# Copying the values' shifted halves on GpSimd instead of by DMA, in an attention kernel followed by a two-layer network

## The chip, the cores and the metric

The kernel runs on one core of a Trainium2 chip. The metric is the device time of one execution, in microseconds (us); a lower time is better. The core has TensorE (PE: matmuls; PEld: its weight loads), VectorE (DVE), ScalarE (ACT), GpSimd (POOL) and SyncE (SP). Transfers are issued from a queue of GpSimd or of SP and run on 16 DMA engines. The working memory (SBUF) has 128 partitions; matmul results lie in PSUM.

## The reference

There are 8 batches, 8 heads, 576 positions and a head size of 64. Heads 0 to 3 attend to the last 32 positions ("plain"); heads 4 to 7 to every fourth of the last 128 ("dilated"). The attention's output, 4608 rows of 512, goes through two matrices with a SiLU between them.

```python
scores = scale * np.matmul(q, k.transpose(0, 1, 3, 2))
rel = pos[:, None] - pos[None, :]
mask_plain = (rel >= 0) & (rel < 32)
mask_dil = (rel >= 0) & (rel < 128) & (rel % 4 == 0)
scores = np.where(masks, scores, -1e9)      # plain: h < 4, dilated: h >= 4
attn = exp(scores - max) / (sum + 1e-9)
x = np.matmul(attn, v)                      # -> (4608, 512)
h = x @ w_in                                # 512 x 2048
out = (h * sigmoid(h)) @ w_out              # 2048 x 512
```

## The kernel before, in words

**Work per batch.** The 576 queries of a head are cut into blocks of 32, each of which sees 64 keys: its own 32 and the 32 before. A dilated head is first split into its four classes of positions modulo 4, after which each class is a plain head of 144 positions. For one batch and one kind of head (z = 0 plain, z = 1 dilated) the steps are: scores (L362 plain, L374 dilated, small matmuls), mask and maximum (L486 to L512, VectorE), exp (L525, L534, ScalarE), normalisation (`normal`, L543 to L550, VectorE), transposing the weights (on TensorE, L559 and L567, or by DMA, L574), `values` (L601 and L665 on TensorE) and `finish`, which puts the result into xT. Then layer 1 (L691 with SiLU at L699) and layer 2 (L756) run over the batch, 16 tiles of the hidden size and 4 or 5 tiles of rows.

**Values.** The tile `vw`, of which there are two (batch b uses `vws[b % 2]`), holds v in pieces of 64 keys on partitions. `load_v` (L158 to L181) brings the pieces from HBM into partitions 64 to 127 (and a short tail). Each piece is needed a second time, shifted by 32 keys, in partitions 0 to 63. These shifted halves are made by `shift_v` (L200), out of four copies within `vw`, each of 32 partitions of 16-bit numbers:

- `shift_class` (L193): 2048 numbers per partition, dilated heads
- `shift_over` (L198): 1024, dilated heads
- `shift_plain` (L186, L188): 2304 and 2048, plain heads

The function is handed the operation that copies. Batch 0 has its own copies (some by DMA from SP, some on VectorE).

**Rows of q and k.** For batches 1 and 2 `load_qk` (L107) loads them and TensorE transposes them. From batch 3 on `load_rows` (L119 plain, L127 dilated; 12 issues on GpSimd) loads them and `cross` (L140, L147) transposes them by DMA, issued from SP.

**Order.** All engines work their own instructions in the order in which the program wrote them. The order is written out by hand in `plan_of(b)`: `at(s, f, ...)` runs f at step s of batch b, where steps 0 to 15 are the tiles of layer 1 and those from 16 the groups of four matmuls of layer 2. Loads of later batches are so placed between the matmuls of this one; the attention of batch b + 1 is computed during the layers of batch b. On GpSimd this gives, in b = 0: v of batch 1, `load_qk(2)` (L107), rows of batch 3, v of batch 2, its shift; in b = 1: v of 3, its shift, rows of 4; from b = 2: v of b + 2, its shift, rows of b + 3. A load of v into a buffer waits until TensorE has done with the batch before in it (L665 is its last use). Batch 1's shift is issued from SP.

Of the kernel before, what the change touches and what calls it, by code (L numbers as in the profile page):

```python
# [29 lines left out]
def kernel(  # L30
# [9 lines left out]
    nc = tc.nc  # L40
    B, H, S, D = q.shape
# [727 lines left out]
    def transposes(at, b, z, step):  # L769
        for which in (1, 0):  # L770
            at(step, transpose, b, z, which, both)

    def later(at, b, z, steps, copies=(nc.vector.tensor_copy, nc.vector.tensor_copy)):

        for hi in (0, 1):
            if steps[hi] is not None:
                at(steps[hi], normal, b, z, hi)
        for hi in (0, 1):
            at(steps[2], turn, b, z, hi)
        for hi in (0, 1):  # L780
            at(steps[2], turned, b, z, hi, copies[hi])
        at(steps[3], values, b, z)
        at(steps[3], finish, b, z, copies)

    def plan_of(b):
        ev = {}

        def at(s, fn, *args):
            ev.setdefault(s, []).append((fn, args))

        def all_exps(b, z):
            for hi in (0, 1):
                at(16, exps, b, z, hi)

        if b == 0:

            at(-16, normal, 0, 1, 1)
            at(-15, shift_class, 0, dve, 1, 2)
            at(-14, normal, 0, 0, 1)
            at(-13, clear_v, 1, nc.vector)  # L800
            at(-13, load_v, 1)
            for c in (2, 3):
                at(-13, load_w_out, c)
            at(-13, load_qk, 2)
            at(-8, turn, 0, 1, 1)
            at(-8, turned, 0, 1, 1, act)
            at(-6, values0, 1, 1)
            at(-6, last_values, 0, 1, (1,))
            at(-6, finish0, 1, 1)
            at(-6, last_finish, 0, 1, 1)  # L810
            at(-4, turn, 0, 0, 1)
            at(-4, turned, 0, 0, 1)
            at(-2, values0, 0, 1)
            at(-2, last_values, 0, 0, (1,))
            at(-2, finish0, 0, 1, both)
            at(-2, last_finish, 0, 0, 1)
            transposes(at, 1, 1, 2)
            at(8, scores, 1, 1)
            for hi in (0, 1):
                at(8, shift, 1, 1, hi)  # L820
            for which in (1, 0):
                at(17, transpose, 1, 0, which, (dve, dve))
            at(20, normal, 1, 1, 0)
            at(20, scores, 1, 0)
            at(14, shift_v, 1, nc.sync.dma_start)
            at(15, load_rows, 3)
            at(15, load_v, 2)
            at(15, shift_v, 2, nc.gpsimd.dma_start)
            all_exps(1, 1)
            for hi in (0, 1):  # L830
                at(20, exps, 1, 0, hi)
            for n, z, hi in ((20, 1, 1), (26, 0, 0), (28, 0, 1)):
                at(n, normal, 1, z, hi)
            for n, z, copies in ((27, 1, (dve, dve)), (30, 0, both)):
                for hi in (0, 1):
                    at(n, turn, 1, z, hi)
                for hi in (0, 1):
                    at(n, turned, 1, z, hi, copies[hi])
                at(n + 1 + z, values, 1, z)
                at(n + 1 + z, finish, 1, z, both)  # L840
        elif b == 1:
            transposes(at, 2, 0, 2)
            transposes(at, 2, 1, 11)
            at(2, cross, 3, 0)
            at(20, cross, 3, 1)
            at(28, cross, 4, 0)
            at(8, scores, 2, 0)
            for hi in (0, 1):
                at(8, shift, 2, 0, hi)
            at(17, load_v, 3)  # L850
            at(17, shift_v, 3, nc.gpsimd.dma_start)
            at(17, load_rows, 4)
            at(14, scores, 2, 1)
            all_exps(2, 0)
            all_exps(2, 1)
            for hi in (0, 1):
                at(21, normal, 2, 0, hi)
            at(21, scores, 3, 0)
            at(21, exps, 3, 0, 0)
            at(21, exps, 3, 0, 1)  # L860
            later(at, 2, 0, (None, None, 27, 28))
            later(at, 2, 1, (29, 31, 33, 34))
        else:
            if b + 2 < B:
                at(16, cross, b + 2, 1)
                at(16, load_v, b + 2)
                at(16, shift_v, b + 2, nc.gpsimd.dma_start)
            if b + 3 < B:
                at(16, load_rows, b + 3)
            if b + 1 < B:  # L870
                if b == 2:
                    later(at, 3, 0, (0, 0, 4, 6))
                else:
                    at(6, values, b + 1, 0)
                    at(6, finish, b + 1, 0)
                at(11, scores, b + 1, 1)
                at(11, shift, b + 1, 1, 1)
                all_exps(b + 1, 1)
            if b + 2 < B:
                at(17, scores, b + 2, 0)  # L880
                for hi in (0, 1):
                    at(18, exps, b + 2, 0, hi)
            if b + 1 < B:
                for hi in (0, 1):
                    at(22 + hi, normal, b + 1, 1, hi)
                    at(22 + hi, turn_by_dma, b + 1, 1, hi)
                at(29, values, b + 1, 1)
                at(29, finish, b + 1, 1)
            if b + 2 < B:
                for hi in (0, 1):  # L890
                    at(27 + hi, normal, b + 2, 0, hi)
                    at(27 + hi, turn_by_dma, b + 2, 0, hi)
            if b + 3 < B:
                at(31, cross, b + 3, 0)

        def plan(s):
            for fn, args in ev.pop(s, ()):
                fn(*args)

        return plan  # L900
# [58 lines left out]
    for b in range(B):  # L959
        plan = plan_of(b)  # L960
        if b == 0:
            for x in range(NFF):
                plan(2 * x - NFF)
                plan(2 * x + 1 - NFF)
                layer1_part(2 * x % NFF, 2 * x // NFF, None if x else warm)
        else:
            for f in range(NFF):
                plan(f)
                layer1(b, f)
        if b == 0:  # L970
            layer2_first(plan)
        else:
            layer2(b, plan)
        for s in range(NFF, 3 * NFF):
            plan(s)
# [30 lines left out]
```

## Time and profile before

| | |
|---|---|
| three runs | 314.29, 315.76, 318.0 us (median 315.76) |
| the profiled execution's own time | 316.22 us |
| its span, first to last instruction | 314.4 us |
| mean granted TensorE clock | 0.977 |
| DMA bytes in all | 41.27 MB, mean 131 GB/s |
| copies within vw, issued from GpSimd | 24 issues; 4.0 to 5.4 us to landing (medians) |
| copies within vw, issued from SP | 7 issues (3 of batch 0, 4 of batch 1); 5.3 to 6.5 us to landing |
| ScalarE, SiLU of layer 1 (L699) | 72.8 us busy |

"Busy" is the time in which an engine had an instruction under way. The chain is the sequence of work that ended last, followed back from the end; its "issue" entries are times in which the engine waited for nothing that the profile shows. In a timeline, `[2.65 <-DMA w_out...]` says that the engine sat idle 2.65 us before the row and what ended this. A queue's share is the time that its packets took, of 16 engines' span; packets of two queues overlap, so shares of a short stretch can add up to more than 100%.

### The profile page before, as it was taken

The page shows a single profiled execution, that of the slowest core. Times are in us where ns is not written, and L with a number is a line of the kernel's source. Part 1 is how long each engine was busy: PE and PEld are TensorE (multiplying, and loading weights), DVE is VectorE, ACT ScalarE, POOL GpSimd, SP SyncE. Part 2 cuts the span into 40 slices and gives each one's busy share as a digit, 9 for nine tenths or more (in the row PEclk, how much of TensorE's full clock was granted, in tenths as well). Part 3 has the DMA queues.
Part 4 walks back from the last instruction along what each step waited for, and adds up shares of the span by engine and source line. Part 5 has one row for each costly group of instructions (what it writes and reads, how often), then busy time and mean ns, then how long its engine had stood idle before and what let it go on. Part 6 is the DMA issues. An engine that isn't in the chain of part 4 may idle for free.

```text
span 314.4 us, 10401 instructions
## 1 busy us (share of the span) xinstructions
PE 298.6 (95%) x4465; PEld 191.3 (61%) x4465; DVE 166.0 (53%) x352; ACT 186.3 (59%) x554; POOL 102.7 (33%) x160
## 2 busy tenths in 40 slices
PE   5789999999999969999989999999999999999995
PEld 2458755677446846467644676467744676467544
DVE  5896588627697334841676126851587034520011
ACT  2775658766992537945694356955695448436300
POOL 8536537715584165056504183042000000000000
PEclk9679999999999989999999999999999999999999
DMA  8999999999999999399996999299715100310021
GB/s 108 188 212 205 191 230 172 170 186 139 171 171 166 189 141 124 93 162 199 123 145 139 176 207 123 76 159 174 106 56 127 67 4 0 109 69 2 0 102 68
DMA packets 105087, 41.27 MB, mean 131 GB/s; under 512 B 79248, under 2 KB 99600, under 8 KB 105040
## 3 DMA queue, kind: packets, MB, share of 16 engines
q0 software_dynamic: 64160, 21.73, 66.8%
q1 hardware_dynamic: 40736, 18.80, 29.2%
q8 instruction: 35, 0.57, 0.7%
q14 instruction: 12, 0.10, 0.1%
q10 hardware_dynamic: 144, 0.07, 0.1%
HBM read 37.75 MB, written 9.44 MB: 150 GB/s over the span
## 4 chain that ended last, share of the span: by engine, by line
PE 85%; DMA 5%; DVE 3%; ACT 3%; issue 2%; POOL 1%; POOLq 0%; DVEq 0%
PE h L691 34%; PE o L756 32%; PE o L730 5%; PE h L711 4%; PE x L601 3%; DMA ptT<-pn 3%; DMA n<-in_q_dram 2%; PE s L374 1%; PE s L362 1%; PE pt L559 1%; PE t L312 1%; ACT pe L534 1%; PE x L627 1%; POOL n L156 1%; DVE ob L740 1%
## 5 line engine op out<-in xcount | busy, mean ns | idle before, releaser
L699 ACT ACTIVATE gT<-h 128x576 f16<-128x576 f32 x112 | 72.8, 650 | 85.8 <-PE h L691 85.6
L691 PE MATMUL h<-xT,w_in 128*128 128x288 f16 x896 | 115.2, 289 | 0.0
L756 PE MATMUL o<-w_out,gT 128*128 128x512 f16 (+1 forms) x528 | 114.1, 373 | 0.0
L691 PEld LDWEIGHTS <-w_in 128*128 128x128 f16 x896 | 87.2, 99 | 24.3 <-DVE xT L678 0.3
L756 PEld LDWEIGHTS <-gT 128*128 128x128 f16 x528 | 50.6, 98 | 54.9
L534 ACT ACTIVATE pe<-ms,nm 128x64 f32<-128x64 f32 x178 | 59.1, 333 | 4.2 <-DVE nm L502 4.1
L740 DVE COPY ob<-o 128x512 f32<-128x512 f32 (+1 forms) x34 | 23.1, 681 | 51.8 <-PE o L756 51.0
L486 DVE SCALAR_TENSOR_TENSOR ms<-s,mask 128x512 f32<-128x512 f32 x28 | 19.2, 685 | 45.6 <-PE s L374 28.3
L534 ACT ACTIVATION_READ_ACCUMULATOR pe<-ms,nm 128x1 f32 x178 | 33.2, 186 | 0.0
L678 DVE CAST xT<-x 128x512 f16<-128x512 f32 x26 | 16.8, 684 | 27.9 <-PE xs L665 27.9
L550 DVE TENSOR_TENSOR pn<-pe,r 128x640 f16<-128x640 f32 (+2 forms) x32 | 25.3, 792 | 1.1
L165 POOL DMA_DIRECT2D vw<-in_v_dram x16 | 10.0, 638 | 44.8 <-PE xs L665 44.6
L502 DVE TENSOR_REDUCE nm<-ms 128x10 f32<-128x640 f32 (+1 forms) x28 | 22.0, 786 | 1.0
L711 PE MATMUL h<-xT,w_in 128*128 128x256 f16 (+1 forms) x128 | 17.4, 290 | 1.0 <-ACT gT L718 1.0
L119 POOL DMA_DIRECT2D n<-in_q_dram x20 | 14.8, 788 | 2.5 <-DMA vw<-vw 2.5
L711 PEld LDWEIGHTS <-w_in 128*128 128x128 f16 x128 | 12.3, 99 | 4.9 <-issue 1.7
L119 POOL DMA_DIRECT2D n<-in_k_dram x20 | 14.8, 759 | 1.4 <-issue 1.3
L730 PE MATMUL o<-w_out,gT 128*128 128x512 f16 x64 | 15.1, 380 | 0.0
L718 ACT ACTIVATE gT<-h 128x512 f16<-128x512 f32 (+1 forms) x16 | 10.3, 650 | 6.9 <-PE h L711 6.8
L601 PEld LDWEIGHTS <-vw 64*64 64x64 f16 x896 | 8.7, 108 | 5.8 <-issue 5.8
L601 PE MATMUL x<-ptT,vw 64*64 64x32 f16 x896 | 10.3, 187 | 0.7 <-DVE ptT L567 0.5
L740 ACT COPY ob_last<-o 128x128 f32<-128x128 f32 x1 | 0.3, 265 | 17.0 <-DMA out_dram<-ob 17.0
(108 smaller groups left out, 258.0 us busy)
## 6 DMA issues: line engine op xcount, KB each, us to landing
out_dram<-ob SPq DMA_DIRECT2D x35, 256.0 KB, 2.3
vw<-in_v_dram POOLq DMA_DIRECT2D x8, 288.0 KB, 8.4
vw<-in_v_dram POOLq DMA_DIRECT2D x16, 128.0 KB, 5.7
w_in<-in_moe_w_in_dram POOLq DMA_DIRECT2D x4, 512.0 KB, 11.8
w_out<-in_moe_w_out_dram POOLq DMA_DIRECT2D x4, 512.0 KB, 10.4
n<-in_k_dram POOLq DMA_DIRECT2D x6, 256.0 KB, 5.5
n<-in_q_dram POOLq DMA_DIRECT2D x6, 256.0 KB, 5.7
vw<-vw POOLq DMA_DIRECT2D x12, 128.0 KB, 4.7
```

What stands on the lines that cost most here:

```text
L119: nc.gpsimd.dma_start(out=f[:, h // 2, :, h % 2], in_=src[b, h].rearrange("(m p) d -> p m d", p=RT))
L486: nc.vector.scalar_tensor_tensor(out=ms[:, 0:8].rearrange("p (n t) c -> p n (t c)", n=2), in0=s[hi].rearrange("p n t c -> p n (t c)"), sca ...
L502: nc.vector.tensor_reduce(out=nm[:, 0:w], in_=ms[:, 0:w], axis=AX.X, op=ALU.max, negate=True)
L534: nc.scalar.activation(pe[:, t, :], slot(t), AF.Exp, scale=1.0 if b else scale, bias=nm[:, t : t + 1], accum_out=l[:, t : t + 1],)
L550: nc.vector.tensor_tensor(pn[:, 0:w], a["pe", z, hi][:, 0:w], r[:, 0:w, None].broadcast_to([P, w, KB]), ALU.mult)
L601: nc.tensor.matmul(dst, w, p, start=True, stop=True)
L691: nc.tensor.matmul(h[:, half, 0:HS], w_in16[:, c, f * P : f * P + P], xT[:, c, half * HS : half * HS + HS], start=(c == 0), stop=(c == MC ...
L699: nc.scalar.activation(gT[:, f, s0 : s0 + S].rearrange("p (a c) -> p a c", a=2), h[:, :, 0:HS], AF.Silu)
L711: nc.tensor.matmul(h[:, i, 0 : c1 - c0], w_in16[:, c, (f + i) * P : (f + i + 1) * P], xT[:, c, c0:c1], start=(c == 0), stop=(c == MC - 1),)
L730: nc.tensor.matmul(o, gT[:, f, t * P : (t + 1) * P], w_out16[:, f, :], start=(f == 0), stop=(f == NFF - 1),)
L740: copy(ob, o)
L756: nc.tensor.matmul(o, gT[:, f, t * P : (t + 1) * P], w_out16[:, f, m0:m1], start=(f == 0), stop=(f == NFF - 1),)
```

## The change

The operation handed to `shift_v` becomes GpSimd's `tensor_copy` for batches 1 to 7; batch 1's copies thereby move from SP to GpSimd, behind `load_qk(2)` and ahead of the rows of batch 3. From b = 1 on the rows of batch b + 3 are issued ahead of these copies instead of behind them. Batch 0 is as it was. The instructions of TensorE, VectorE and ScalarE, and their order, are the same.

```diff
-            at(14, shift_v, 1, nc.sync.dma_start)
+            at(14, shift_v, 1, nc.gpsimd.tensor_copy)
             at(15, load_rows, 3)
             at(15, load_v, 2)
-            at(15, shift_v, 2, nc.gpsimd.dma_start)
+            at(15, shift_v, 2, nc.gpsimd.tensor_copy)
...
             at(17, load_v, 3)
-            at(17, shift_v, 3, nc.gpsimd.dma_start)
             at(17, load_rows, 4)
+            at(17, shift_v, 3, nc.gpsimd.tensor_copy)
...
                 at(16, load_v, b + 2)
-                at(16, shift_v, b + 2, nc.gpsimd.dma_start)
-            if b + 3 < B:
-                at(16, load_rows, b + 3)
+                if b + 3 < B:
+                    at(16, load_rows, b + 3)
+                at(16, shift_v, b + 2, nc.gpsimd.tensor_copy)
```

The copies themselves are unchanged:

```python
def shift_plain(b, copy, m0, m1):
    f = vws[b % 2][:, 0:NP].rearrange("p (h m) d -> p h m d", h=HH)
    copy(out=f[W:KB, :, m0:m1], in_=f[KB : KB + W, :, m0:m1])
    l0 = max(m0, 1)
    copy(out=f[0:W, :, l0:m1], in_=f[KB + W : P, :, l0 - 1 : m1 - 1])

def shift_class(b, copy, m0, m1):
    vw = vws[b % 2]
    copy(out=vw[W:KB, NP + m0 * ND : NP + m1 * ND], in_=vw[KB : KB + W, NP + m0 * ND : NP + m1 * ND])

def shift_over(b, copy):
    vw = vws[b % 2]
    copy(out=vw[0:W, NP + ND : NP + 2 * ND], in_=vw[KB + W : P, NP : NP + ND])
```

## The prediction, written before the changed kernel ran

> **What bounds the kernel now.** I read the page first (busy times, the DMA queues, the chain's shares), then the chain in order of time, then GpSimd's timeline, and last the places where TensorE first uses the copied values.
>
> From the page: spans, queues (packets, MB, share of 16 engines) and the chain's shares.
>
> ```profile
> PE 298.6 (95%) x4465; PEld 191.3 (61%) x4465; DVE 166.0 (53%) x352; ACT 186.3 (59%) x554; POOL 102.7 (33%) x160
> q0 software_dynamic: 64160, 21.73, 66.8%
> q1 hardware_dynamic: 40736, 18.80, 29.2%
> q8 instruction: 35, 0.57, 0.7%
> PE 85%; DMA 5%; DVE 3%; ACT 3%; issue 2%; POOL 1%; POOLq 0%; DVEq 0%
> ```
>
> TensorE is busy 298.6 of 314.4 us: whatever is not hidden under it costs its full length, and at most 15.8 us can be gained, most of it before 23 us and after 309 us, which this change does not touch. q0 and q1 together take 96% of the 16 DMA engines' span, and the traffic lies almost wholly before 244 us; so transfers queue until then.
>
> From the chain in order of time (start, us, what), the breaks of TensorE between 60 and 300 us:
>
> ```profile
> 75.30 0.13 issue
> 112.43 2.53 issue
> 115.43 6.68 PE h L691 x40
> 156.54 1.64 issue
> 188.05 0.29 issue
> ```
>
> They lie in the middle of a run of equal score matmuls, with nothing that the profile shows to wait for. Counting TensorE's records, weight loads included, 1280 lie from the second to the third and 768 from the third to the fourth: multiples of 256. q8 brought 0.57 MB in 35 packets, 16 KB each. I read the breaks as late blocks of TensorE's own instructions, held up behind data in the DMA engines. After the second the clock granted in 116 to 120 us was 0.58, and the 40 matmuls behind it took 6.68 us where the same 40 take 5.01 elsewhere. So this cause costs 0.13 + 2.53 + 1.67 + 1.64 + 0.29 = 6.3 us. [...]
>
> GpSimd's timeline, the rows that anchor the sums (start, us, engine, line, what, [idle before]):
>
> ```profile
> 0.24 0.10 POOL L990 MEMSET const-float32-0.0<- 128x1 f32 x1 [0.24 <-issue]
> 2.74 0.24 POOL masks.py:197 MEMSET ident<- 128x128 f16 x1
> 3.06 0.29 POOL masks.py:199 TENSOR_SCALAR_AFFINE_SELECT ident<-ident 128x128 f16<-128x128 f16 x1
> 3.31 0.23 POOL L243 TENSOR_SCALAR_AFFINE_SELECT band<-band 32x64 f32<-32x64 f32 x1
> ...
> 47.95 0.56 POOL L107 DMA_DIRECT2D n<-in_q_dram  x1 [2.65 <-DMA w_out<-in_moe_w_out_dram]
> 48.90 1.50 POOL L119 DMA_DIRECT2D n<-in_k_dram  x2 [0.39 <-issue]
> ...
> 74.34 0.49 POOL L186 DMA_DIRECT2D vw<-vw  x1 [4.16 <-DMA vw<-in_v_dram]
> ...
> 97.94 1.22 POOL L165 DMA_DIRECT2D vw<-in_v_dram  x2 [4.32 <-PE xs L665]
> ```
>
> and TensorE's first uses of shifted values of batch 1 (plain heads) and batch 3:
>
> ```profile
> 57.23 0.59 PEld L601 LDWEIGHTS <-vw 64*64 64x64 f16 x64 [0.42 <-issue]
> ```
> ```profile
> 106.17 0.69 PE L601 MATMUL x<-ptT,vw 64*64 64x32 f16 x64
> ```
>
> GpSimd is one queue: it issues every load in program order and waits in that order. Up to batch 3 it has little idle time; from 97.94 us on it sits idle each batch until TensorE frees the values' buffer (4.3 us there, by the waits 44.6 us in four times, the longest 15.1).
>
> **What is removed.** Six sets of four DMA issues on GpSimd (0.52 + 0.53 + 0.49 + 0.58 = 2.1 us a set) and one set on SP at 38.3 to 42.7 us, with the wait for their loads ahead of them. 475 KB a set go from the DMA engines: 32 partitions x 7424 elements x 2 bytes; seven sets are 3.3 of 41.3 MB, 8%. Nothing on SP waits behind its set (its next issue is at 54.83), so that costs and gains nothing there.
>
> **What is added: the price of a set on GpSimd.** The trace has no GpSimd copy. The slope between the two selects is (0.287 - 0.229) / 64 = 0.9 ns an element with 0.17 us fixed; between the two memsets (0.24 - 0.10) / 127 = 1.10 ns with 0.10 fixed. Middle: 1.02 ns and 0.13 us. 2048 + 1024 + 2304 + 2048 = 7424 elements and four instructions give 8.1 us a set. Low end: VectorE's own copy of this kind, 32x1024 in 0.416 us, 0.41 ns: 3.0 us. High end: the 128-element select taken as all slope, 0.287 / 128 = 2.2 ns: 16.6 us. I take 8.1, since two independent GpSimd slopes lie beside it. [...]
>
> **What moves, set by set.**
> Batch 1: the set starts when the loads ahead end, 47.95 + 0.56 = 48.5, and ends at 56.6. The class heads (their two copies done by 51.9) are first used at 54.1, the plain heads at 57.23: covered with 0.6 us to spare. Beyond that TensorE waits one for one.
> Rows of batch 3 sit behind it: 8 + 4 issues now at 48.9 to 58.0 come at 56.6 to 65.2. The first half's q then lands near 67.5 (4.9 us for L119), its transposes on SP end near 72.5 and land some 8 to 9 later, 81; the scores of batch 3 start at 82.55. Covered with about 1.5. SP's stores behind these transposes are not due before 82.5.
> Batch 2: its values' loads move from 57.9-63.4 to 65.2-70.7. Their landing (10.9 us after the issue for the plain part, 74.3 now) gives 81.6; the two plain copies, 4.7 us, end at 86.3. First used at 90.2: covered with 3.9.
> Batch 3: its values' loads follow (75.45-79.0 now, then 86.3-89.9), the rows of batch 4 next (8.6 us of issue, to 98.5), then the set, to 106.6. First use 106.17: 0.4 us late. This is the chain that decides: three sets in one queue, so each us more per set makes it 3 us later. Batch 4's values and batch 5's rows follow at 106.6 to 118.8, not later than now (114.0 to 122.4 for the rows); the rows of batch 4 come 5 us later on SP than now (91.72), 25 us ahead of their scores at 122.97.
> Batches 4 to 7: rows are issued right behind the values' loads, in b = 3 at 138.9 to 147.5 instead of 145.2 to 156.8; the set then ends near 155.6, and the values are first used at 181.7. All covered by the idle time that the rows above show.
>
> **Instruction blocks.** The traffic falls by 8%, but rows now run beside the transposes of q and k. For the break at 156.54 the rows in flight end some 9 us earlier, so it should shrink; the boundary 256 records earlier, near 149.7, now has them in flight and no break today. I set these against each other: 0. Bounds: -6.3 (all gone) and +6.3 (as many again).
>
> **Sum**, against the profiled execution, 316.22 us with a span of 314.4: 316.22 + 0.4 (batch 3) + 0 (batches 1, 2, 4 to 7) + 0 (blocks) = 316.6; rounded up, 317, as the unknowns above lie further out than those below. The three runs have a median of 315.76 and a spread of 314.29 to 318.0, so the profiled one is 0.46 above the median and I do not correct for it. About 1% (3.2 us) is what a measurement of this kernel can tell from no change.
>
> **The rivals.**
> 1. GpSimd is slower than the slopes say: slower. With C us a set, batch 3 is 0.4 + 3 x (C - 8.1) late. It decides from C = 9.1 on (317 + 3). At 11 us, TensorE gets its values 9 us late: 326; at 16.6 us, 26 late: 342. For it: selects and memsets are not copies, and nothing of this length ran on GpSimd. Against: two slopes agree. Chance 0.25.
> 2. Copy and VectorE exclude each other while both read: slower. In 48.5 to 56.6 VectorE has three multiplies with both inputs in SBUF (L550: 0.82, 0.69, 0.82), which feed TensorE's transposes at 51.5 and 55.6; in 98.5 to 106.6 two more (0.69, 0.82). If they take turns, the first set ends 2.3 later (1.7 past its use), each multiply waits about half a copy, 1 us, and the third set ends 3.8 later, of which about 2 remain: 317 + 1.7 + 1 + 2 = 321.7. The trace shows no GpSimd operation that reads SBUF beside such a multiply, for or against. [...] Chance 0.2.
> 3. The blocks come in time: faster. Lighter queues end most of the 6.3 us: two thirds gone is 312.4, all gone 310.4. For it: all four breaks lie where the queues are full. Against: 8% is little, and the earlier rows fill the queue elsewhere. Chance 0.17.
> 4. The copies are no copies on GpSimd, or the order is another: the program's order on GpSimd shows the 28 copies and the rows ahead of them, and those of the other compute engines do not change; set aside.
>
> **How the numbers follow.** Forecast (within 1%) 0.38, its own range 314 to 320; slower 0.25 + 0.2 = 0.45; faster 0.17. The range 312 to 327 takes in two thirds of the gain of rival 3, all of rival 2, and rival 1 up to 11.3 us a set; I leave about 0.07 below and 0.11 above.
>
> **What would show it.** GpSimd copies of L193, L198, L186 and L188 at about 2.2, 1.2, 2.5 and 2.2 us each (8.1 a set); the first set at 48 to 57; the third ending near 106.6, just at the use of batch 3; no wait of TensorE at 57 and at 143.5 and 181.7; breaks named issue again some 6 us in all, one of them near 149.7 and less at 156. It is wrong if a set takes over 9.1 us, if L550 shows waits ended by GpSimd, if batch 3's values come over 3 us late, or if the breaks add up to less than 3 us.

## The result, and the profile after

| | before | after |
|---|---|---|
| median, us (runs) | 315.08 (314.29 to 318.0; 4) | 330.53 (326.95 to 331.74; 4) |
| profiled execution, us | 316.22 | 329.79 |
| its span, us | 314.4 | 328.0 |

The ratio is 1.0454 [1.0345, 1.0563]: slower by 4.5%, 13.5 us above the forecast and 3.5 above the top of its range. (Ratios leave out runs over 1.5% above the fastest of their kernel, so one need not be the quotient of two medians; the profiles of experiments 3, 4, 8, 9 and 10 are of such a run, and single waits read in them need not stand in the others.)

The page of after, lines that answer to those of before (busy time of the engines, the two large queues, the chain's shares, the group of the multiply that `normal` ends with):

```profile
PE 304.5 (93%) x4465; PEld 194.3 (59%) x4465; DVE 177.2 (54%) x352; ACT 186.4 (57%) x554; POOL 140.4 (43%) x164
q0 software_dynamic: 63104, 18.88, 61.3%
q1 hardware_dynamic: 40448, 18.33, 27.6%
PE 80%; DVE 13%; issue 3%; ACT 2%; POOL 1%; DMA 0%; POOLq 0%; DVEq 0%
L550 DVE TENSOR_TENSOR pn<-pe,r 128x640 f16<-128x640 f32 (+2 forms) x32 | 30.3, 947 | 1.1
```

The queues carry the 3.3 MB less that the change promised. But VectorE, given the same 352 instructions, is busy 11.2 us longer (166.0 before), and its share of the chain went from 3% to 13%. L550 alone grew from 25.3 to 30.3 us; its line of the page before:

```profile
L550 DVE TENSOR_TENSOR pn<-pe,r 128x640 f16<-128x640 f32 (+2 forms) x32 | 25.3, 792 | 1.1
```

In the groups by line, L547 (a very small addition) grew from 5.7 to 8.6 and L512 (an addition of the negated maximum) from 7.1 to 10.0: with L550, 10.8 of the 11.2 us.

GpSimd's timeline of after, the first set and the end of the third (start, us, engine, line, what, [idle before]):

```profile
47.81 1.88 POOL L193 COPY vw<-vw 32x2048 f16<-32x2048 f16 x1
49.75 1.03 POOL L198 COPY vw<-vw 32x1024 f16<-32x1024 f16 x1
50.84 2.10 POOL L186 COPY vw<-vw 32x2304 f16<-32x2304 f16 x1
53.00 2.37 POOL L188 COPY vw<-vw 32x2048 f16<-32x2048 f16 x1
...
103.18 2.37 POOL L188 COPY vw<-vw 32x2048 f16<-32x2048 f16 x1
```

VectorE's timeline of before has the two instructions that matter most here at their usual length:

```profile
50.94 0.82 DVE L550 TENSOR_TENSOR pn<-pe,r 128x640 f16<-128x640 f32 x1
51.68 0.17 DVE L547 TENSOR_SCALAR r<-l 128x8 f32<-128x8 f32 x1
```

VectorE's timeline of after, beside these copies:

```profile
51.22 2.40 DVE L550 TENSOR_TENSOR pn<-pe,r 128x640 f16<-128x640 f32 x1
53.54 1.86 DVE L547 TENSOR_SCALAR r<-l 128x8 f32<-128x8 f32 x1
...
101.28 2.52 DVE L550 TENSOR_TENSOR pn<-pe,r 128x640 f16<-128x640 f32 x1
103.73 0.68 DVE L740 COPY ob<-o 128x512 f32<-128x512 f32 x1
```

Read the two together. L550 starts at 51.22, while copy L186 (50.84 to 52.94) is under way. It ends at 53.62, 0.68 after the copy's end, and needs 0.82 when it is alone. The small L547 behind it takes 1.86 us instead of 0.17: it ends at 55.40, and copy L188 ends at 55.37. The copy L188 itself took 2.37 instead of 1.88, since L550 was at work in its first 0.6 us. So these instructions of the two engines take turns, each for its whole length. Not every VectorE instruction waits: L740 at 103.73, which reads PSUM, takes its usual 0.68 us in the middle of a copy.

TensorE's timeline of after, the three places where this reached it (the second through the copy of L325, which stood behind the additions of L512), and the matmuls behind the last:

```profile
53.68 0.45 PE L559 MATMUL pt<-ident,pn 128*128 128x128 f16 x5 [0.81 <-DVE pn L550]
...
79.68 0.68 PE L374 MATMUL s<-kC,qC 64*32 64x64 f16 x64 [1.41 <-DVE qC L325]
...
103.86 0.45 PE L559 MATMUL pt<-ident,pn 128*128 128x128 f16 x5 [3.28 <-DVE pn L550]
...
105.30 1.07 PE L601 MATMUL x<-ptT,vw 64*64 64x32 f16 x64
```

After the wait of 3.28 us the clock granted in 104 to 108 us was 0.61 (1.00 in the same stretch of before), and 64 matmuls took 1.07 us, where 63 such take 0.70 at 57 us.

The chain of after in order of time: VectorE's addition in the second set, and the breaks behind 120 us:

```profile
74.52 3.77 DVE ms L512 x2
...
121.92 2.54 issue
124.94 6.68 PE h L691 x40
...
159.39 1.41 issue
...
198.19 2.58 issue
201.17 6.33 PE h L691 x40
```

Where the 13.6 us of the profiled execution arose can be read from TensorE's work, which is the same in both:

| TensorE's work | start before | start after | later by |
|---|---|---|---|
| values of batch 1, dilated (L601) | 54.18 | 57.22 | 3.0 |
| scores, plain (L362) | 67.68 | 70.78 | 3.1 |
| scores, dilated (L374) | 75.44 | 79.68 | 4.2 |
| values of batch 2, plain (L601) | 90.64 | 94.91 | 4.3 |
| values of batch 2, dilated (L601) | 97.23 | 105.38 | 8.2 |
| values of batch 3, plain (L601) | 106.23 | 115.63 | 9.4 |
| scores, dilated (L374) | 149.21 | 158.69 | 9.5 |
| values (L601) | 168.84 | 178.96 | 10.1 |
| layer 2 (L756) | 193.63 | 207.50 | 13.9 |
| end of layer 2 | 309.33 | 322.75 | 13.4 |

Two causes stand apart. By 116 us, in the sets of batches 1 to 3, TensorE fell 9.4 us behind through VectorE's waits: 3.0 in the first set (0.3 of it stood before the first copy), 1.2 in the second, 5.1 in the third, of which some 1.5 is the low clock. From 150 us on, some 4 us more came with breaks in the middle of equal matmuls: 1.41 us at 159.39, a place that had none before (149.9 there), and 2.58 at 198.19 (0.29 at 188.05 before), with a slow stretch of 6.33 instead of 5.01 us behind it; against these the break at 167.62 is down to 0.67 from 1.64.

### The profile page after: what moved, and what is told of

Same layout as the page of the kernel before. It is cut to its first block, busy times and chain, and to the rows that moved or that the text cites. A ratio compares the mean times of both kernels' runs of the same rounds, so it can differ in the third digit from the quotient of the medians.

```text
span 328.0 us, 10390 instructions
## 1 busy us (share of the span) xinstructions
PE 304.5 (93%) x4465; PEld 194.3 (59%) x4465; DVE 177.2 (54%) x352; ACT 186.4 (57%) x554; POOL 140.4 (43%) x164
## 3 DMA queue, kind: packets, MB, share of 16 engines
q0 software_dynamic: 63104, 18.88, 61.3%
q1 hardware_dynamic: 40448, 18.33, 27.6%
## 4 chain that ended last, share of the span: by engine, by line
PE 80%; DVE 13%; issue 3%; ACT 2%; POOL 1%; DMA 0%; POOLq 0%; DVEq 0%
PE h L691 33%; PE o L756 30%; PE h L711 5%; DVE pn L550 3%; PE x L601 3%; PE s L374 2%; DVE ms L512 1%; DVE nm L502 1%; DVE ms L486 1%; PE o L730 1%; PE s L362 1%; DVE r L547 1%; DVE l L543 1%; ACT pe L534 1%; PE pt L559 1%
## 5 line engine op out<-in xcount | busy, mean ns | idle before, releaser
L691 PE MATMUL h<-xT,w_in 128*128 128x288 f16 x896 | 116.5, 291 | 0.0
L756 PE MATMUL o<-w_out,gT 128*128 128x512 f16 (+1 forms) x528 | 115.2, 375 | 0.0
L691 PEld LDWEIGHTS <-w_in 128*128 128x128 f16 x896 | 87.8, 99 | 25.0 <-DVE xT L678 0.3
L756 PEld LDWEIGHTS <-gT 128*128 128x128 f16 x528 | 50.9, 98 | 55.5 <-issue 1.1
L740 DVE COPY ob<-o 128x512 f32<-128x512 f32 (+1 forms) x34 | 23.1, 680 | 51.9 <-PE o L756 50.9
L550 DVE TENSOR_TENSOR pn<-pe,r 128x640 f16<-128x640 f32 (+2 forms) x32 | 30.3, 947 | 1.1
L711 PE MATMUL h<-xT,w_in 128*128 128x256 f16 (+1 forms) x128 | 18.4, 303 | 0.0
L193 POOL COPY vw<-vw 32x2048 f16<-32x2048 f16 x7 | 13.2, 1881 | 6.2 <-DMA vw<-in_v_dram 6.0
L711 PEld LDWEIGHTS <-w_in 128*128 128x128 f16 x128 | 12.9, 104 | 4.3 <-issue 0.5
L186 POOL COPY vw<-vw 32x2304 f16<-32x2304 f16 x7 | 14.7, 2098 | 1.7 <-DMA vw<-in_v_dram 1.3
L188 POOL COPY vw<-vw 32x2048 f16<-32x2048 f16 x7 | 14.7, 2094 | 0.4
```

The lines of the kernel that those rows point to most:

```text
L550: nc.vector.tensor_tensor(pn[:, 0:w], a["pe", z, hi][:, 0:w], r[:, 0:w, None].broadcast_to([P, w, KB]), ALU.mult)
L691: nc.tensor.matmul(h[:, half, 0:HS], w_in16[:, c, f * P : f * P + P], xT[:, c, half * HS : half * HS + HS], start=(c == 0), stop=(c == MC ...
L711: nc.tensor.matmul(h[:, i, 0 : c1 - c0], w_in16[:, c, (f + i) * P : (f + i + 1) * P], xT[:, c, c0:c1], start=(c == 0), stop=(c == MC - 1),)
L740: copy(ob, o)
L756: nc.tensor.matmul(o, gT[:, f, t * P : (t + 1) * P], w_out16[:, f, m0:m1], start=(f == 0), stop=(f == NFF - 1),)
```

## The experiments

Two theories, by the letters that the expectations use. A: a GpSimd copy and certain VectorE instructions exclude each other, as long as the one that started first runs. C: the new order (rows straight behind the values' loads) delays blocks of TensorE's instructions. The rival at hand, B: GpSimd's time in its queue decides, because the copies are too slow or come too late for the values. Each ratio is against runs of the kernel before on the same chip.

### 1. Memsets in place of the copies

```diff
+    def blank(out, in_):
+        nc.gpsimd.memset(out, 0.0)
-            at(14, shift_v, 1, nc.gpsimd.tensor_copy)
+            at(14, shift_v, 1, blank)
```

And so in the three other places; the shifted halves are zeros in this kernel.

> This kernel leaves out the shifted halves of the values of batches 1 to 7: in the changed kernel, each of the 28 GpSimd copies is replaced by a GpSimd memset of the same destination, so GpSimd writes as much, for about as long (1.1 ns per element by the memset row, 8 us a set), in the same place of its queue, but reads nothing from SBUF. Theory A (a GpSimd copy and a VectorE operation with two SBUF inputs exclude each other while both read; 9.4 of the 13.6 us): L550 falls from a mean of 0.947 us back to 0.79, no L550 of 2.4 us or more, and the time is that of the kernel before plus what the instruction blocks cost more, 315 to 320. Rival B (the time goes because GpSimd's queue is held and loads come late, whatever it executes): 327 to 332, as the changed kernel.

320.87 us, ratio 1.0169 [1.0079, 1.026], a little above what was expected. The memsets took 1.80, 0.94 and 2.01 us, within 10% of the copies. In the timelines (line numbers 3 higher in this kernel):

```profile
47.62 6.70 POOL L201 MEMSET vw<- 32x2048 f16 x4
...
50.46 2.05 DVE L550 TENSOR_SCALAR r<-l 128x10 f32<-128x10 f32 x1
...
52.79 0.83 DVE L553 TENSOR_TENSOR pn<-pe,r 128x640 f16<-128x640 f32 x1
```

The multiply with two inputs is back at 0.83 us beside a memset (group: 25.3 us, as before), and so is the addition (7.1 us). The small TENSOR_SCALAR, with one input, still waits: 2.05 us here, 9.8 us in the group (5.7 before). So it is not the time on GpSimd as such that holds the two-input instructions, but that the GpSimd instruction reads SBUF: the multiply that took 2.40 us beside a copy takes 0.83 beside a memset of nearly the same length. The TENSOR_SCALAR is held by one that only writes, too; why it and the two-input instructions differ here is not shown. TensorE still waited 1.61 us in the first set, and breaks remained (2.31 at 152.85); how much of this kernel's 5 us over before is such waits and how much breaks was not taken apart.

### 2. Copies on GpSimd for batches 4 to 7 alone

```diff
-                at(16, shift_v, b + 2, nc.gpsimd.dma_start)
-            if b + 3 < B:
-                at(16, load_rows, b + 3)
+                if b + 3 < B:
+                    at(16, load_rows, b + 3)
+                at(16, shift_v, b + 2, nc.gpsimd.tensor_copy)
```

> Only batches 4 to 7 are copied by GpSimd, with the rows ahead of them; batches 1 to 3 as before. Theory A: the long waits of VectorE (51 to 58, 74 to 78, 97 to 104 us) belong to the sets of batches 1 to 3, which fall into the normalisations that TensorE waits for; without them L550 and L512 in those places take 0.8 us again, and the time is 315 plus at most the 4.2 us more of instruction blocks: 315 to 320. Rival (each of the seven sets costs about the same, 13.6 / 7 = 1.9 us): 315 + 7.8 = 323.

318.8 us, 1.0108 [1.0019, 1.0197]. L550's group is at 25.3 us and L512's at 7.1, as before; L547's still grew, to 7.8. The exclusion costs where VectorE is normalising or masking at that moment for a matmul soon due, as in batches 1 to 3; the later sets fall beside other work. Breaks of 1.20 (149.55) and 2.03 us (188.14) came with the order of the rows.

### 3. The order alone, with the DMA shifts

The rows of batch b + 3 go ahead of the shift from b = 1 on; the shift stays a DMA.

> The order alone: rows of q and k ahead of the shifts from b = 1 on, shifts by DMA as before. If the 4 us that the blocks of instructions cost more in the changed kernel come from rows that now run beside the transposes (theory C), the breaks named issue in the chain add up to 8 to 11 us and the time is 317 to 320. If the order costs nothing, 314 to 316 and breaks of about 6 us. Theory A expects no long L550 here.

322.36 us, 1.019 [1.0064, 1.0316]. No VectorE group changed (25.3, 5.9, 7.1 us). Breaks of 1.94, 2.33, 1.72 and 2.79 us at 99.57, 117.99, 153.63 and 191.89, with two shorter ones 9.7 us in all, as expected, and a mean clock of 0.972 (0.977 in before). The order costs by itself, as C says, and 2 us more than C expected.

### 4. The copies of after in quarters

```diff
+    def in_four(out, in_):
+        n = out.shape[1] // 4
+        for i in range(4):
+            nc.gpsimd.tensor_copy(out=out[:, i * n : (i + 1) * n], in_=in_[:, i * n : (i + 1) * n])
-            at(14, shift_v, 1, nc.gpsimd.tensor_copy)
+            at(14, shift_v, 1, in_four)
```

And so in the three other places.

> The changed kernel with every GpSimd copy cut into four copies of a quarter (112 copies in all); by two rows of it (1.88 us for 2048, 1.03 for 1024) a copy has 0.18 us fixed, so a set takes 7424 x 0.83 ns + 16 x 0.18 = 9.1 us instead of 7.1. Theory A, with the exclusion lasting for one instruction: a VectorE operation waits at most 0.6 us instead of 2.1, so the 9.4 us fall to about 3, and the time to 321 to 326. Rival B (GpSimd's time in the queue decides): 2 us more per set in series of three, 334 to 337.

316.88 us over 10 runs, 1.005 [1.0013, 1.0087]: better than either theory expected. A copy of a quarter takes 0.61 us on the mean, and the first set 10.27 us in all instead of 7.6; yet beside it VectorE waits far less:

```profile
51.63 1.08 DVE L555 TENSOR_TENSOR pn<-pe,r 128x640 f16<-128x640 f32 x1
52.63 0.63 DVE L552 TENSOR_SCALAR r<-l 128x8 f32<-128x8 f32 x1
```

The same two took 2.40 and 1.86 us in after. The two-input groups are nearly back (26.4 us for the multiply, 7.2 for the addition of L512); the small addition's group is not (8.7 us, as in after), but in short waits. What costs is the length of one GpSimd instruction, not the sum; that GpSimd is slow, or late (B), is refuted, since here it is slower and later and the time is 13.7 us lower. That is more than the 9.4 us of the waits: most of what the order cost has gone as well, and why is open.

### 5. The copies of batches 2 to 7 on VectorE

```diff
-            at(15, shift_v, 2, nc.gpsimd.dma_start)
...
-            at(17, shift_v, 3, nc.gpsimd.dma_start)
+            at(15, shift_v, 2, dve)
...
-                at(16, shift_v, b + 2, nc.gpsimd.dma_start)
+                at(1 if b == 2 else 3, shift_plain, b + 1, dve, 0, NM)
+                at(8, shift_class, b + 1, dve, 0, 2)
+                at(8, shift_over, b + 1, dve)
```

> The copies of batches 2 to 7 on VectorE instead, put where VectorE is idle in the profile before (batch 2 at step 15 of b = 1; later batches at steps 1 or 3 and 8 of the batch before), batch 1 by DMA from SP and the rows' order as before. By VectorE's own copy, 32x1024 in 0.416 us, a set takes at most 3.0 us. Theory A and the blocks: no wait between GpSimd and VectorE of more than a DMA issue, lighter queues, and GpSimd's loads no longer held up by the wait for the values: 311 to 316. Rival (VectorE's own time comes back in the normalisations): 6 sets of 3 us, partly on the path, 318 to 325.

320.97 us, 1.0208 [1.0126, 1.029]: expectation missed. The copies are short (2048 numbers in 0.68 to 0.77 us) and no VectorE group waits. But GpSimd now has no shift to wait for, so the rows follow straight behind the values' loads (rows of batch 6 from 141.46 us, 145.20 in before), and breaks of 2.07, 1.83, 1.33, 0.95 and 2.58 us stand in the chain. VectorE's share of the chain is 1%, so its own time, the rival here, is not what came back. I read this so: the wait for the values' landing, which shift and copy have in common when the rows stand behind them, was holding the rows back.

### 6. The instruction blocks themselves

Before, with 28 more matmuls and their 28 weight loads at the very front of TensorE's stream, 56 records; nothing else.

```diff
-    keep_busy(big.tile([P, 2, 512], F32, tag="big", name="busy"), 4)
+    busy = big.tile([P, 2, 512], F32, tag="big", name="busy")
+    for _ in range(32):
+        nc.tensor.matmul(busy[:, 0, 0:64], ident, ident[:, 0:64], start=True, stop=True)
```

> The kernel before with its four warm-up matmuls of 512 columns replaced by 32 of 64 columns, which adds 28 matmuls and 28 weight loads to the front of TensorE's stream, at the same TensorE time. Theory of blocks: the breaks named issue still come at records that are 193 above a multiple of 256, counted from the new start, so 56 records (28 matmuls) earlier in the work: the long break near 112 us after 24 instead of 52 matmuls of that run of scores. Time 314 to 318. Rival (the breaks belong to the score matmuls or to their operands): they stay at the same matmul, 52 into the run.

318.81 us, 1.0171 [1.009, 1.0252]. In before the break near 112 us (112.43 in the chain) lies behind 52 of 64 equal matmuls:

```profile
111.92 0.51 PE s L374 x52
```

Here, in TensorE's timeline:

```profile
117.27 0.36 PE L374 MATMUL s<-kC,qC 64*32 64x64 f16 x24
118.31 0.48 PE L374 MATMUL s<-kC,qC 64*32 64x64 f16 x40 [0.68 <-issue]
```

24 is 52 less 28: the break moved by just the records added. In every profile here the breaks lie at records that leave 193 when divided by 256 (matmuls, weight loads and semaphore records counted). So they are tied to a place in the instruction stream.

The packets of q8 in the traces show what ends a break. There are 35 of 16 KB, one for every 256 of TensorE's records (8949 in before and in after). In all 14 profiles no boundary from 193 + 2 x 256 on was passed sooner than 1.2 us after the end of its packet, and each of the 63 breaks of over 0.1 us at one ended 1.2 to 2.1 us after it (in before: packet to 113.40, break to 114.96). What differs is how late the packet comes. The one for the break at 159.39 of after started 5.1 us after TensorE had passed the boundary before; the same one in before started after 1.7 us, and there was no break. Which transfers held it up is not shown.

The time was above what was expected; the moved boundaries have breaks in new places, 1.37 us at 48.49 and 1.26 at 220.76.

### 7 and 8. The copies with the rows behind them, as before

Before with `in_four` in place of the four DMA shifts, and with the whole copy in their place; the order of before.

> GpSimd copies in quarters, as in the split kernel (316.9), but the rows of q and k behind them, as in the kernel before. If the order costs by itself (the order alone measured 322.4 with the DMA copies, 7 us), this is 2 to 5 us below the split kernel: 312 to 315, with fewer breaks near 148 and 190. If the order costs only together with DMA copies, it is 316 to 318, and the rows may come too late behind the wait for the values.

> The changed kernel without its other part: whole copies on GpSimd, rows behind them as before. Theory A with its 9.4 us for the exclusion, which does not depend on the order for batch 1 (3 us) and little for batches 2 and 3: 322 to 328. If the order were the larger part, 315 to 319.

Quarters: 318.75 us, 1.0149 [1.0077, 1.0221]; missed. Rows went out at 129.55 us, beside the weights' DMA transposes, for which the chain waits twice (4.01 and 4.72 us). Whole copies: 324.63 us, 1.0226 [1.013, 1.0323]; as expected, with waits in L550 (28.9 us) and L547 (9.7) and none in L512 (7.1). The six combinations, ratio to before:

| shift | rows behind | rows ahead |
|---|---|---|
| DMA | 1 | 1.019 [1.0064, 1.0316] |
| GpSimd, whole | 1.0226 [1.013, 1.0323] | 1.0454 [1.0345, 1.0563] (after) |
| GpSimd, quarters | 1.0149 [1.0077, 1.0221] | 1.005 [1.0013, 1.0087] |

Whole copies and order each cost about 2%, together 4.5: within the intervals they add up. In the last row the order gains about 1% instead of losing, though the two intervals just touch. So its price is not a constant; that it depends on what else lies in the queues when the rows go out is argued, not shown.

### 9 to 11. The rows in the quiet stretch

If late blocks are the trouble, the rows of batches 6 and 7 might go ahead of the values' loads, where the queues are less full (DMA share in before 0.61 in 122 to 134 us and 0.76 in 158 to 168, against 1.98 in 145 to 157 and 1.83 in 182 to 191; packets that overlap are added up).

```diff
+                if b > 2 and b + 3 < B:
+                    at(16, load_rows, b + 3)
                 at(16, load_v, b + 2)
                 at(16, shift_v, b + 2, nc.gpsimd.dma_start)
-            if b + 3 < B:
-                at(16, load_rows, b + 3)
+                if b == 2:
+                    at(16, load_rows, b + 3)
```

Experiment 9 is this in before; 10 has, besides, copies in quarters for batches 4 to 7; 11 is after with this order.

> The kernel before with one change of order: the rows of batches 6 and 7 are issued ahead of the values' loads of batches 5 and 6 instead of behind their shift, and so run in the stretches of 122 to 134 and about 158 to 168 us, in which the DMA engines are lightly used, instead of beside the transposes at 145 to 157 and 182 to 191. Theory C (rows beside the transposes make TensorE's instruction blocks late): the breaks near 150 to 158 and 188 shrink from 1.9 us in all to under 0.5, time 1 to 3 us below the kernel before. If the rows' place does not matter for the blocks: as before, within 1 us.

> As the last, and with the shifts of batches 4 to 7 made by GpSimd copies in quarters; batches 1 to 3 by DMA as before. Theory A: these sets lie where TensorE waits for no normalisation, so the exclusion costs under 1 us; with 1.9 MB less for the DMA engines the blocks come no later: 1 to 4 us below the kernel before. Rival (a GpSimd copy costs wherever it lies): 2 us above.

> The changed kernel with the rows of batch 5 behind the copies again and those of batches 6 and 7 in the quiet stretches (batch 4's as in the changed kernel). Theories A and C together: the exclusion's 8 to 9 us stay, the order's 6 go: 322 to 326. If the order had no part in the changed kernel's loss, 330.

320.71 us, 1.0157 [1.0106, 1.0209]; 322.61, 1.0247 [1.0212, 1.0282]; 327.75, 1.0401 [1.0347, 1.0454]. The first two missed by sign, the third by a little. The break near 188 is gone in 9, but its chain now has

```profile
133.10 5.62 DMA ptT<-pn
...
170.18 6.60 DMA ptT<-pn
```

The weights' DMA transposes, which landed after 2.4 us in before (median of all 18), now took 5.5. In 10 the median is 4.2, and the chain has waits of 7.24 and 7.36 us for them. In 11 hardly a break is left (0.53 us at 79.00), but the waits for VectorE remain (30.5 us of L550), and TensorE waits 1.58 and 2.97 us for these transposes near 141: fewer breaks alone do not bring the time back.

### 12. The rows between the two halves of the copies

Batches 1 to 3 as before. From b = 2 on: values' loads, the dilated heads' copies in quarters on GpSimd (they wait for their loads), the rows, the plain heads' copies in quarters.

```diff
-                at(16, shift_v, b + 2, nc.gpsimd.dma_start)
-            if b + 3 < B:
-                at(16, load_rows, b + 3)
+                at(16, shift_class, b + 2, in_four, 0, 2)
+                at(16, shift_over, b + 2, in_four)
+                if b + 3 < B:
+                    at(16, load_rows, b + 3)
+                at(16, shift_plain, b + 2, in_four, 0, NM)
```

> Batches 1 to 3 as before. From b = 2 on: values' loads, the dilated heads' copies in quarters on GpSimd, the rows, then the plain heads' copies in quarters. The rows are so issued near 147 and 182, about where the kernel before issues them, after the values have landed and ahead of the transposes of the weights. If the place of the rows and the exclusion are all that the change costs, and the lighter DMA queues all that it gains (1.9 of 41.3 MB here), this is 0 to 3 us below the kernel before: 312 to 315. If GpSimd copies beside VectorE still cost, or the rows still make blocks late: 316 to 319.

313.86 us over 12 runs against 314.86 over 17: 0.9973 [0.9932, 1.0014], as expected. It cannot be told from before, but beats after by 16.7 us. Page and GpSimd's timeline:

```profile
PE 89%; DMA 3%; DVE 3%; ACT 2%; issue 1%; POOL 1%; POOLq 0%; DVEq 0%
```
```profile
140.81 2.63 POOL L203 COPY vw<-vw 32x512 f16<-32x512 f16 x6 [1.28 <-DMA ptT<-pn]
143.40 2.94 POOL L119 DMA_DIRECT2D n<-in_k_dram  x4
```

The rows start behind the first values' landing and the weights' transposes, no break of over 0.2 us stands in the chain after 115 us, the transposes land in 2.5 us (median), the multiply's group is at 25.4 us and the mean clock at 1.000.

## Why the prediction was wrong, point by point

- **The step that failed: the sum "316.22 + 0.4 (batch 3) + 0 (batches 1, 2, 4 to 7) + 0 (blocks)".** It holds no term for copy and VectorE excluding each other, which was rival 2 with a chance of 0.2. That mechanism was the larger part: 9.4 of 13.6 us (table above), shown by experiments 1 and 4. With the order as before (experiment 8), whole copies cost 1.3 to 3.2%, 4 to 10 us.
- **Rival 2 was itself too small, 321.7.** It counted the multiply L550 alone and "about half a copy, 1 us" for each. Measured: 1.6 to 1.7 us for each of three multiplies (51.22, 97.55 and 101.28, 0.82 alone; the last two are those at 93.36 and 94.55 of before, not those that the rival named); L547 waits too, 1.7 us at 53.54, and the addition L512, 3.77 us in the chain for two (0.68 and 0.82 alone) in the second set, where the rival saw nothing. And a wait of TensorE of 3.28 us was followed by a clock of 0.61 in 104 to 108 us, which the rival left out. The sum of its terms on the path was 4.7; measured 9.4.
- **"Instruction blocks … I set these against each other: 0."** The reading of the breaks as blocks was right (experiment 6), and so was the place: one came at the boundary "near 149.7", and the one at 156.54 shrank. But they did not cancel. The shrinkage was 1.0 us; the new break, the larger one at 188 and the clock behind it cost 1.4 + 2.3 + 1.3 = 5.0. The net of 4.0 lies within the stated bounds of ±6.3; the middle had no measured support.
- **"Batch 3's set ends … 106.6 … This is the chain that decides."** The third set ended at 105.55, near the figure, but partly by luck: a set takes 6.9 us by itself, and waits for loads (3.61 and 1.31 us in the second set) and for VectorE made up the rest. And it decided nothing, since VectorE's waits made the values' use 9 us later.
- **The price of a set, 8.1 us.** Measured 1.88 + 1.03 + 2.10 + 1.89 = 6.9 us undisturbed (rows of the fourth set, the last at 126.36 us): (1.88 - 1.03) / 1024 = 0.83 ns an element and 0.18 us fixed. The selects and memset gave 1.02 ns, too high. Rival 1 (slower GpSimd) is refuted.
- **Right:** batches 4 to 7 are covered (experiment 2: L550 and L512 as before), and the queues' bytes fell as worked out (21.73 to 18.88 MB and 18.80 to 18.33). Rival 3, a gain from lighter queues, did not occur in after.

Open: why the order of the rows costs 2% with DMA shifts or whole copies and gains with quarters. The DMA bytes moved are the same for whole and quartered copies, so bytes alone do not explain it. How much of experiment 3's loss is breaks and how much low clock was not separated.

## What to carry to other kernels

Before a GpSimd instruction is put beside VectorE work that feeds the bounding engine, list VectorE's instructions in that window by their inputs: those that took turns here, with two inputs in SBUF or the small TENSOR_SCALAR, waited for a whole GpSimd instruction (2.40 and 1.86 us beside whole copies, 1.08 and 0.63 beside quarters), so the longest single instruction is what counts; cut it up (quarters took the loss from 4.5% to 0.5%) or move it to where VectorE has slack. A wait on a queue may be what spaces out the transfers behind it: when it is removed, look for what now collides with them. In a kernel whose bounding engine streams short instructions, read breaks that nothing explains against the count of instructions, and a row set at "these cancel" by its bounds.

## What the runs showed of the hardware that was not expected

- A VectorE TENSOR_SCALAR on 10 numbers a partition, 0.18 us alone, took 2.05 us beside a GpSimd memset, which reads nothing.
- VectorE copies 2048 16-bit numbers a partition in 0.7 us, GpSimd in 1.88; a quarter of it, 512, takes GpSimd 0.64 on the mean, more than 1.88 / 4 = 0.47.
- Three breaks of TensorE in after, of 2.5 to 3.3 us, are each followed by a granted clock of 0.57 to 0.67 over the next 4 us; behind two of them 40 matmuls took 6.33 and 6.68 us instead of 5.01. Length alone does not decide: in experiment 5 a break of 1.83 us at 116.27 was followed by a clock of 0.57, one of 2.58 us at 192.09 by 1.00. In after the low stretches behind these breaks last 3.41 us each and start multiples of that apart (104.85, 125.33 and 200.43). Counted on in such steps from 118.66, where the low stretch of experiment 5 starts, the shorter break lay within one step (115.25 to 118.66, TensorE busy for 1.58 us of it) and the longer one across the step at 193.74; that this decides is not shown.
- A 16 KB packet of instructions that comes late stops TensorE until 1.2 to 2.1 us after the packet's end (63 breaks in 14 profiles).
